# Routed expert rows on one Trainium2 core: fetches that wait for fewer scatters, and padding rows moved from behind each list to ahead of it

## The chip, the cores and the metric

One core of one Trainium2 chip runs the kernel. The metric is the device time of one execution in microseconds (us). A core has five engines that matter here: TensorE (PE, matmuls; its weight loads are listed as PEld), VectorE (DVE), ScalarE (ACT), GpSimd (POOL) and SyncE (SP). Each engine runs its own instructions strictly in the order in which the program holds them, and waits for others at semaphores. SP computes nothing here: it issues most of the DMA transfers. POOL issues the DMAs whose row addresses are computed on the chip.

## The reference

```
# x: 8 x 3584 tokens of 192;  weight_gen: 8 heads x 7 taps for each token
w = softmax(weight_gen, axis=-1)
x = einsum('bshk,bskhg->bshg', w, windows(x_pad, 7))   # causal mix of 7 tokens
x = x.reshape(N, D)                                     # N = 28672, D = 192

xn = x / (norm(x) + 1e-6);  en = expert_emb / (norm(expert_emb) + 1e-6)
logits = xn @ en.T / tau                                # 8 experts
expert_idx = argmax(logits);  gate_w = softmax(logits)[expert_idx]
for e in range(8):
    mask = expert_idx == e
    h = maximum(x[mask] @ w1[e], 0)                     # 192 -> 1024
    out[mask] = gate_w[mask] * (h @ w2[e])              # 1024 -> 192
```

Each token goes through one expert alone, so the kernel sorts the tokens by expert before the two large matmuls.

## The kernel before

**Chunks.** The 28672 tokens are worked in 16 chunks of 1792 (14 groups of 128). For each chunk SP loads the tokens (`x_t`, two loads of 1248 KB) and the tap weights (`w_t`, 392 KB); DVE and ACT mix the seven taps; the chunk's rows (`row`) are turned by a transposing DMA (`xT<-row`), TensorE forms the logits (`g_ps`), and DVE finds each token's expert and its place (`pos`) in that expert's list. Then POOL writes the chunk's rows into the lists with 14 indirect DMAs, the scatters (`lst<-row,pos`, 128 rows of 776 bytes each, L590). `lst` lies in DRAM: a region of REG = N + 256 rows for each of the 8 experts, and a few rows of zeros behind them all (row DUMMY and on), which a tile reads that has nothing to do. `run` holds for each expert where the next row goes, `used` where the next row to be read lies.

**Tiles.** With each of the chunks 0 to 14 go eight tiles, one for each expert, of 128 or 256 rows (`sizes`, L25): 120 tiles, numbered here from 0, so that chunk c has tiles 8c to 8c+7. `schedule` (L612) decides on DVE whether the expert's list has enough rows by then. Behind them come 45 "last" tiles of 128 rows, whose experts and rows a plan on the chip picks (class `Plan`, around L836) from what the lists still hold. A tile's fetch (`load_rows` and `fetch`, L643 to L661) is three steps on SP: read the first row's number from `sched` into a register (TENSOR_LOAD), a transposing DMA `xt<-lst`, and a small DMA `meta<-lst` with the gates and token numbers. There are three `xt` buffers (`XBUFS`), so a fetch waits at least until TensorE has done the first matmuls of the tile three before it. TensorE then does `first` (`h_ps<-xt,wall`), ACT and DVE the two halves of the ReLU (`hi`, `lo`), TensorE `second` (`acc<-wall,hi` and `lo`), ACT scales, and POOL stores the tokens' results (`out_dram<-o,meta`).

**Order.** The program is emitted by a planner (`run_steps`, L942) that holds costs and priorities for steps; a framework adds the semaphores from the tiles and the DRAM tensors that instructions touch. It sees `lst` as one tensor. So the kernel takes dependences away by groups: scatters are in the group "rows", fetches in the group "loads", and an instruction can be declared free of a whole group. In the kernel before, scatters are declared free of both groups, while a fetch keeps its dependence on every scatter that the program emitted ahead of it, of its own chunk or of a later one.

**Padding.** A last tile always reads 128 rows, so it can reach beyond its list's end. `pads` (L1346) writes 256 rows of zeros behind each list's last row when the last chunk has been placed: eight times a register load and a DMA of 194 KB on SP, ahead of the last tiles' fetches. At the very start `pad_rows` (L1055) writes the rows at DUMMY. A fallback behind the program (from L1480) takes what 45 last tiles did not; it is not run with these inputs.

Of the kernel before, what the change touches and what calls it, by code (L numbers as in the profile page):

```python
# [11 lines left out]
I32 = mybir.dt.int32  # L12
AF = mybir.ActivationFunctionType
ALU = mybir.AluOpType
# [78 lines left out]
def tile_dynconv_moe(  # L93
# [535 lines left out]
    class Tile:  # L629
# [13 lines left out]
        def load_rows(self, row0, deps):  # L643
            def fetch():
                return self.fetch(nc.sync.value_load(row0, min_val=0, max_val=DUMMY))

            for i in SP.behind(fetch):
                i = raw_ins(i)
                tc.add_to_no_dep_group("loads", i)
                for d in deps:  # L650
                    tc.add_manual_dep(i, d.name, sync_dep, reason="rows of the lists")

# [129 lines left out]
    class Plan:  # L782
# [27 lines left out]
        def make(self):  # L810
            E1 = E + 1
            jt, ji = self.take(M), self.take(M, dt=I32)
            G_.iota(ji, pattern=[[1, M]], base=0, channel_multiplier=0)
            G_.tensor_copy(out=jt, in_=ji)
            left, lefti = self.take(E), self.take(E, dt=I32)
            V.tensor_tensor(out=left, in0=run[0:1, :], in1=used, op=ALU.subtract)
            yield
            V.tensor_scalar(out=lefti, in0=left, scalar1=float(P - 1), scalar2=None, op0=ALU.add)
            yield
            V.tensor_scalar(  # L820
                out=lefti, in0=lefti, scalar1=P.bit_length() - 1, scalar2=None, op0=ALU.logical_shift_right
            )
            yield
            V.tensor_copy(out=left, in_=lefti)
            ends = self.take(E1)
            V.memset(ends[:, 0:1], 0.0)
            yield
            V.tensor_tensor_scan(
                out=ends[:, 1:], data0=left, data1=zero_t[0:1, 0:E], initial=0.0, op0=ALU.add, op1=ALU.add
            )  # L830
            yield
            past = self.take(M, E1)
            V.tensor_tensor(
                out=past, in0=jt.unsqueeze(2).broadcast_to([1, M, E1]), in1=ends.unsqueeze(1).broadcast_to([1, M, E1]),
                op=ALU.is_ge,
            )  # L836
            first = self.take(E)
            yield
            V.scalar_tensor_tensor(out=first, in0=ends[:, 0:E], scalar=-float(P), in1=used, op0=ALU.mult, op1=ALU.add)
            mine = self.take(M, E)  # L840
            yield
            V.tensor_tensor(out=mine, in0=past[:, :, 0:E], in1=past[:, :, 1:], op=ALU.subtract)
            ex = self.take(M)
            yield
            V.tensor_reduce(out=ex, in_=past[:, :, 1:], axis=AX.X, op=ALU.add)
            self.experts = self.take(M, dt=I32)
            yield
            V.tensor_scalar(out=self.experts, in0=ex, scalar1=float(E - 1), scalar2=None, op0=ALU.min)
            num = self.take(E)
            yield  # L850
            V.tensor_reduce(out=num, in_=mine.rearrange("p m e -> p e m"), axis=AX.X, op=ALU.add)
            yield
            V.scalar_tensor_tensor(out=used, in0=num, scalar=float(P), in1=used, op0=ALU.mult, op1=ALU.add)
            yield
            V.tensor_tensor(out=mine, in0=mine, in1=first.unsqueeze(1).broadcast_to([1, M, E]), op=ALU.mult)
            rows = self.take(M)
            yield
            V.tensor_reduce(out=rows, in_=mine, axis=AX.X, op=ALU.add)

            yield  # L860
            V.tensor_scalar(
                out=jt, in0=jt, scalar1=float(P), scalar2=-float(DUMMY), op0=ALU.mult, op1=ALU.add
            )
            yield
            V.scalar_tensor_tensor(out=jt, in0=past[:, :, E], scalar=-1.0, in1=jt, op0=ALU.add, op1=ALU.mult)
            self.rows = self.take(M, dt=I32)
            yield
            V.scalar_tensor_tensor(
                out=self.rows, in0=rows, scalar=float(DUMMY), in1=jt, op0=ALU.add, op1=ALU.subtract
            )  # L870
# [16 lines left out]
    e_i = prep.tile([P, E], I32, name="e_i")  # L887
    G_.iota(e_i, pattern=[[1, E]], base=0, channel_multiplier=0)
    V.tensor_copy(out=rev[:, 0, :], in_=e_i)
    V.tensor_scalar(out=run, in0=rev[:, 0, :], scalar1=float(REG), scalar2=None, op0=ALU.mult)  # L890
    V.tensor_scalar(out=rev, in0=rev, scalar1=-1.0, scalar2=float(E), op0=ALU.mult, op1=ALU.add)
    V.tensor_copy(out=used, in_=run[0:1, :])
    wlast = prep.tile([P, WC], F16, name="wlast")
# [23 lines left out]
    def add(eng, cost, fn, deps=(), key=(), dma=0.0, lat=1.0):  # L917
        s = Step(eng, cost, fn, [d for d in deps if d is not None], key, dma, lat)
        steps.append(s)
        return s  # L920
# [134 lines left out]
    def pad_rows():  # L1055
        for r in range(DUMMY, DUMMY + TAIL, P):
            SP.dma_start(out=lst[r : r + P, :], in_=pad)

    L["pads"] = add("SP", 1.0, pad_rows, (), (0, 5), 0.6)

    def taus():
# [281 lines left out]
            t.needs = ([L["parts", e, 0], L["parts", e, 1]], [L["low", e]])  # L1343
            tile_graph(t, (lambda t=t: t.load(scheds[c], routes[c].rows), L["scatter"  , c] + [L["sched", c][-1], L["pads"]]), c)

    def pads(deps):  # L1346

        ends = sm.tile([1, E], I32, name="ends")
        V.tensor_copy(out=ends, in_=run[0:1, :])
        yield  # L1350
        for e in range(E):

            def put():
                r = nc.sync.value_load(ends[0:1, e : e + 1], min_val=e * REG, max_val=e * REG + N)
                return SP.dma_start(
                    out=lst[bass.ds(r, TAIL), :].rearrange("(s p) c -> p s c", p=P),
                    in_=pad.unsqueeze(1).broadcast_to([P, TAIL // P, ROW // 2]),
                )

            i = raw_ins(SP.behind(put))  # L1360
            tc.declare_no_dep(i, group="rows", reason="behind the last token's row")
            tc.declare_no_dep(i, group="loads", reason="behind the rows that are read")
            tc.add_to_no_dep_group("rows", i)
            deps.append(i)

    def last_batch():
        c = NCH - 1
        deps = []
        box = []

        def start():
            box.append(Plan())
            deps.extend(routes[c].rows)
            return box[0].make()

        free_ = [L["taps", (c, u)][-1] for u in range(2)]
        free_ += L["split", (c, 1)] + L["scatter", c] + [L["logits", 2 * c + 1]]
        rows_at = chain(
            lazy(lambda: pads(deps)), [("V", 0.08), ("SP", 8.0)], [last_places(c)[2], L["pads"]], (0, -1, c)
        )  # L1380
        rows_at[1].dma = 0.6
        mk = chain(
            lazy(start), [("V", x) for x in (0.1, 0.08, 0.08, 0.12, 0.08, 0.36, 0.08, 0.33, 0.33, 0.1, 0.33, 0.08, 0.33, 0.33, 0.1, 0.1, 0.1)], [last_places(c)[-1], L["sched", c - 1][-1]] + free_, (1, c, 5)
        )
        nb = 3
        cps = []
        for j in range(M):
            lasts.append(LastBox())
            t = lasts[j]
            t.j = j  # L1390
            k0 = [mk[9], mk[16]]
            prev = cps[-1:]
            old1 = [tile_steps[TB + j - nb]["first"][-1]] if j >= nb else free_
            old2 = [tile_steps[TB + j - nb]["second"][-1]] if j >= nb else free_
            c1 = add("V", 1.12, lambda t=t: t.copy(0), k0 + prev + old1, (1, c, 6, j))
            c2 = add("V", 0.85, lambda t=t: t.copy(1), k0 + [c1] + old2, (1, c, 6, j))
            cps += [c1, c2]
            t.needs = ([c1], [c2])
            t.start(box)
            tile_graph(t, (lambda t=t: t.load(box[0], deps), L["scatter", c] + [mk[16], rows_at[1]]), c)  # L1400

    class LastBox:

# [48 lines left out]
    def fetch_first():  # L1452
# [17 lines left out]
    total = sm.tile([1, 1], F32, name="total")  # L1470
    V.tensor_reduce(out=total, in_=left, axis=AX.X, op=ALU.add)
    lefti = sm.tile([1, E + 1], I32, name="lefti")
    V.tensor_scalar(out=lefti[:, 0:E], in0=left, scalar1=float(TAIL - 1), scalar2=None, op0=ALU.add)
    V.tensor_copy(out=lefti[:, E:], in_=total)
    V.tensor_scalar(
        out=lefti[:, 0:E], in0=lefti[:, 0:E], scalar1=TAIL.bit_length() - 1, scalar2=None, op0=ALU.logical_shift_right
    )
    nexti = sm.tile([1, E], I32, name="nexti")
    V.tensor_copy(out=nexti, in_=used)
    some = nc.values_load(lefti[0:1, E : E + 1], min_val=0, max_val=N)  # L1480
    with tc.If(some > 0):
        for e in range(E):
            n = nc.values_load(lefti[0:1, e : e + 1], min_val=0, max_val=N // TAIL)
            r0 = nc.sync.value_load(nexti[0:1, e : e + 1], min_val=e * REG, max_val=e * REG + N)
            with tc.For_i(0, n, 1) as i:
                t = Tile(e, TAIL)
                t.fetch(nc.s_assert_within(r0 + i * TAIL, e * REG, e * REG + N))
                for g in range(t.ng):
                    t.first(g)
                    t.relu(g)  # L1490
# [58 lines left out]
```

## Time and profile before

| | |
|---|---|
| median of 3 runs | 1243.48 us (1241.87 to 1247.8) |
| profiled execution, its own time | 1246.79 us |
| its span in the trace | 1245.0 us |
| mean granted clock of TensorE | 0.987 |
| PE busy | 1177.2 us (95%) |
| DVE busy | 1066.5 us (86%) |
| ACT busy | 776.1 us (62%) |
| POOL busy | 624.3 us (50%) |

The span is the time from the first to the last instruction of the profiled execution, and the execution's own time is 1.8 us more. Busy time is counted for each engine by itself; issuing DMAs does not count as busy, so SP has no row. A granted clock below 1 means that the hardware let TensorE run at less than its full speed for a part of the time.

### The profile page before, as it was taken

Reading aid. Unit: us, or ns where it says so; the run is one execution under the profiler, and the core shown is the slowest. Engines: PE = TensorE matmul, PEld = TensorE weight load, DVE = VectorE, ACT = ScalarE, POOL = GpSimd, SP = SyncE. Lnnn points to the kernel's source line nnn. Section 1 sums busy time; section 2 is a strip of 40 time slices with the busy share of each in tenths; the row PEclk is TensorE's granted clock in tenths of the full one; section 3 lists DMA queues with packets and bytes.
Section 4 is the critical chain, followed back from the end, with each engine's and each line's share of the span. In section 5 each row is a group of like instructions: output and inputs, shape, how many; then the busy total and the mean of one; then the engine's idle time right before and its main releaser. Section 6 shows DMA issues by size and latency. Waiting matters only on the chain.

```text
span 1245.0 us, 34972 instructions
## 1 busy us (share of the span) xinstructions
PE 1177.2 (95%) x13600; PEld 1050.8 (84%) x13600; DVE 1066.5 (86%) x1505; ACT 776.1 (62%) x1938; POOL 624.3 (50%) x498
## 2 busy tenths in 40 slices
PE   2999979899999999999999899989999999999997
PEld 1554459799988989999898899989999999999997
DVE  5998899799989998999899899988899447778784
ACT  1398867668787877788677678655455533333332
POOL 1006334547555674848284746584848463333332
PEclk9999999999999999999999999999999999999999
DMA  9644554758386747655656657365554541222221
GB/s 368 261 105 119 154 134 113 157 121 181 114 173 160 176 120 162 165 123 152 129 141 139 163 129 176 107 164 128 124 106 98 110 136 46 48 48 50 45 45 32
DMA packets 273487, 162.56 MB, mean 131 GB/s; under 512 B 249493, under 2 KB 258957, under 8 KB 268192
## 3 DMA queue, kind: packets, MB, share of 16 engines
q1 hardware_dynamic: 250416, 101.26, 36.7%
q0 software_dynamic: 21744, 44.30, 11.9%
q10 hardware_dynamic: 1152, 14.68, 2.8%
q8 instruction: 108, 1.77, 0.6%
q14 instruction: 67, 0.55, 0.2%
HBM read 62.24 MB, written 46.55 MB: 87 GB/s over the span
## 4 chain that ended last, share of the span: by engine, by line
PE 57%; DMA 13%; issue 12%; DVE 10%; POOL 6%; ACT 1%; POOLq 0%; SPq 0%; ACTq 0%; DVEq 0%
PE h_ps L78 28%; PE acc L78 22%; DMA lst<-row,pos 5%; PE sums L78 5%; POOL out_dram L78 4%; DMA xT<-row 3%; DVE acc L78 3%; DVE prod L78 3%; POOL lst L78 2%; DMA xt<-lst 2%; DMA out_dram<-o,meta 1%; PE less L78 1%; DMA w_t<-in_weight_gen_dram 1%; PE g_ps L78 1%; DVE lo L78 1%
## 5 line engine op out<-in xcount | busy, mean ns | idle before, releaser
L78 POOL DMA_INDIRECT out_dram<-o,meta x229 | 302.3, 1320 | 407.5 <-ACT o L78 363.6
L78 PE MATMUL h_ps<-xt,wall 128*128 128x256 f16 (+1 forms) x4800 | 458.5, 250 | 26.3 <-DMA xt<-lst 26.3
L78 PEld LDWEIGHTS <-wall 128*128 128x128 f16 (+1 forms) x4996 | 397.3, 99 | 70.8 <-DMA xt<-lst 23.1
L78 ACT ACTIVATE hi<-h_ps 128x512 f16<-128x512 f32 x458 | 272.6, 596 | 266.3 <-PE h_ps L78 190.1
L78 POOL DMA_INDIRECT lst<-row,pos x224 | 313.0, 1397 | 190.1 <-ACT sq L78 95.9
L78 PE MATMUL acc<-wall,hi 128*128 128x192 f16 x2944 | 390.7, 247 | 0.0
L78 PE MATMUL acc<-wall,lo 128*128 128x192 f16 x1472 | 363.4, 247 | 0.0
L78 PEld LDWEIGHTS <-hi 128*128 128x128 f16 x3664 | 330.8, 98 | 17.9 <-issue 0.8
L78 DVE TENSOR_TENSOR prod<-x_t,w_t 128x1344 f32<-128x1344 f32 x178 | 276.1, 1551 | 5.5 <-PE sums L78 3.3
L78 DVE TENSOR_TENSOR acc<-acc,prod 128x1344 f32<-128x1344 f32 x162 | 251.6, 1553 | 2.4
L78 DVE SCALAR_TENSOR_TENSOR lo<-h_ps,hi 128x512 f16<-128x512 f32 x230 | 153.5, 683 | 41.6 <-ACT hi L78 41.6
L78 PEld LDWEIGHTS <-lo 128*128 128x128 f16 x1832 | 179.8, 98 | 0.1
L78 ACT ACTIVATE lo<-h_ps 128x512 f16<-128x512 f32 x228 | 133.7, 594 | 52.3 <-PE h_ps L78 51.5
L78 ACT ACTIVATE o<-acc,meta 128x192 f32<-128x192 f32 x229 | 89.5, 420 | 64.6 <-PE acc L78 54.3
L78 ACT ACTIVATE acc<-acc,sc 128x192 f32<-128x192 f32 x224 | 90.8, 450 | 0.5
L78 ACT ACTIVATE sq<-acc 128x192 f16<-128x192 f32 x224 | 80.9, 361 | 7.0 <-DVE acc L78 4.3
L78 PE MATMUL h_ps<-hi,minus 128*128 128x512 f16 x228 | 84.6, 383 | 0.0
L78 PE MATMUL h_ps<-xt,x_t 128*128 128x128 f16 x1200 | 76.8, 219 | 0.0
L78 PE MATMUL sums<-acc,io_i 128*128 128x448 f32 x114 | 50.7, 584 | 23.1 <-DVE enorm L78 21.1
L78 DVE TENSOR_TENSOR acc<-x_t,w_t 128x1344 f32<-128x1344 f32 x46 | 71.1, 1548 | 1.2 <-PE sums L78 1.1
L78 PEld LDWEIGHTS <-x_t 128*128 128x128 f16 x1200 | 71.1, 98 | 0.0
L78 DVE TENSOR_TENSOR row<-acc,row 128x896 f16<-128x896 f32 x64 | 52.7, 852 | 13.0 <-ACT row L78 12.5
(147 smaller groups left out, 1052.1 us busy)
## 6 DMA issues: line engine op xcount, KB each, us to landing
x_t<-in_x_dram SPq DMA_DIRECT2D x32, 1248.0 KB
wall<-in_moe_w_dram ACTq DMA_DIRECT2D x7, 1792.0 KB
w_t<-in_weight_gen_dram SPq DMA_DIRECT2D x16, 392.0 KB
out_dram<-o,meta POOLq DMA_INDIRECT x229
lst<-row,pos POOLq DMA_INDIRECT x224
xt<-lst SPq DMA_TRANSPOSE x165
wlast<-in_moe_w_dram ACTq DMA_DIRECT2D x1, 1792.0 KB
meta<-lst SPq DMA_DIRECT2D x101, 1.0 KB
```

What stands on the lines that cost most here:

```text
L78: self.last = self.tc.keep_in_program_order(op(*args, **kwargs))
```

## The change

A fetch is declared free of the group "rows", except for the scatters that it names itself, those of its own chunk. Each list now begins 128 rows into its region (`run` starts at e*REG + 128). The last tiles are counted from a list's end: tile j of an expert reads the 128 rows that end 128*j rows ahead of the list's last row, so that the one that doesn't fill up reaches back into rows that were already worked (and writes their results again) or into the 128 rows ahead of the list. Those are filled with zeros by one DMA, `front_rows` (128 x 8 x 194 words, 794 KB), which keeps a dependence on the last scatter of chunk 8; `pads` and its eight DMAs are gone. The planner gives `front_rows` out behind the fetch of tile 76 and the scatters of chunk 8. The fallback goes in tiles of 128 instead of 256.

```
@@ load_rows
             for i in SP.behind(fetch):
                 i = raw_ins(i)
                 tc.add_to_no_dep_group("loads", i)
+                tc.declare_no_dep(
+                    i, group="rows", keep=list(deps), reason="later rows lie behind those that are read"
+                )
                 for d in deps:
                     tc.add_manual_dep(i, d.name, sync_dep, reason="rows of the lists")
@@ Plan
-            V.scalar_tensor_tensor(out=first, in0=ends[:, 0:E], scalar=-float(P), in1=used, op0=ALU.mult, op1=ALU.add)
+            V.scalar_tensor_tensor(
+                out=first, in0=ends[:, 0:E], scalar=float(P), in1=run[0:1, :], op0=ALU.mult, op1=ALU.add
+            )
...
-    V.tensor_scalar(out=run, in0=rev[:, 0, :], scalar1=float(REG), scalar2=None, op0=ALU.mult)
+    V.tensor_scalar(out=run, in0=rev[:, 0, :], scalar1=float(REG), scalar2=float(P), op0=ALU.mult, op1=ALU.add)
@@ behind pad_rows
+    def front_rows():
+        i = raw_ins(
+            SP.behind(
+                SP.dma_start,
+                out=lst[0:DUMMY, :].rearrange("(e r) c -> r e c", e=E)[0:P],
+                in_=pad.unsqueeze(1).broadcast_to([P, E, ROW // 2]),
+            )
+        )
+        r = routes[8].rows[-1]
+        tc.declare_no_dep(i, group="rows", keep=[r], reason="ahead of the first token's row")
+        tc.declare_no_dep(i, group="loads", reason="ahead of the rows that are read")
+        tc.add_manual_dep(i, r.name, sync_dep, reason="in the middle of the run")
+        tc.add_to_no_dep_group("rows", i)
+        front.append(i)
@@ last_batch (def pads is removed)
-            deps.extend(routes[c].rows)
+            deps.extend(routes[c].rows + front)
...
-        rows_at = chain(
-            lazy(lambda: pads(deps)), [("V", 0.08), ("SP", 8.0)], [last_places(c)[2], L["pads"]], (0, -1, c)
-        )
-        rows_at[1].dma = 0.6
+        fronts = add("SP", 1.0, front_rows, [L["pads"], tile_steps[76]["fetch"]] + L["scatter", 8], (1, 76, 1), 0.6)
...
-            tile_graph(t, (lambda t=t: t.load(box[0], deps), L["scatter", c] + [mk[16], rows_at[1]]), c)
+            tile_graph(t, (lambda t=t: t.load(box[0], deps), L["scatter", c] + [mk[16], fronts]), c)
```

The programs' own order shows two places on SP. A wait on DMASW with a number is one for a DMA that POOL issued (a scatter or a store), on DMAHW for one that SP issued, on PE, DVE or Activation for that engine. The first place is tiles 75 to 77 of chunk 9, before: the end of tile 75's fetch, the next chunk's two loads, and the fetches of tiles 76 and 77.

```order
L78 DMA meta<-lst 128x2 [waits DMAHW7_49]
L78 DMA x_t<-in_x_dram 128x2496 [waits DVE_49]
L78 DMA w_t<-in_weight_gen_dram 128x784 [waits DMAHW1_49]
L645 TENSOR_LOAD sched
L645 ISA x2
L78 ISA
L78 DMA_TRANSPOSE xt<-lst 128x3x128 [waits DMAHW2_49,DMASW6_49,PE_49]
L78 ISA
L78 DMA meta<-lst 128x2 [waits DMAHW3_49,DMASW5_49,DMASW4_49]
```

The same place of the changed kernel:

```order
L78 DMA meta<-lst 128x2 [waits DMAHW0_49]
L78 DMA x_t<-in_x_dram 128x2496 [waits DVE_49]
L78 DMA w_t<-in_weight_gen_dram 128x784 [waits DMAHW2_49]
L645 TENSOR_LOAD sched
L645 ISA x2
L78 ISA
L78 DMA_TRANSPOSE xt<-lst 128x3x128 [waits DMAHW3_49,PE_49]
L78 ISA
L78 DMA meta<-lst 128x2 [waits DMAHW4_49,DMASW5_49,DMASW4_49]
```

The order is the same, and the transposing fetch has lost its wait on DMASW6, a scatter of chunk 10. The second place is tiles 58 to 60 of chunk 7, before: the end of tile 58's fetch, a load of tokens, tile 59's fetch, the tap weights of the chunk after next, tile 60's fetch.

```order
L78 DMA meta<-lst 128x2 [waits DMAHW3_49]
L78 DMA x_t<-in_x_dram 128x2496 [waits DMAHW4_49,DVE_49]
L645 TENSOR_LOAD sched
L645 ISA x2
L78 ISA
L78 DMA_TRANSPOSE xt<-lst 128x3x128 [waits DMAHW5_49,DMAHW6_49,DMASW2_49,PE_49]
L78 ISA
L78 DMA meta<-lst 128x2
L78 DMA w_t<-in_weight_gen_dram 128x784 [waits DMAHW7_49]
L645 TENSOR_LOAD sched
L645 ISA x2
```

The same place of the changed kernel, where the DMASW1 of the padding write is chunk 8's last scatter:

```order
L78 DMA meta<-lst 128x2 [waits DMAHW3_49]
L78 DMA x_t<-in_x_dram 128x2496 [waits DMAHW4_49,DVE_49]
L645 TENSOR_LOAD sched
L645 ISA x2
L78 DMA lst<-pad 128x8x194 [waits DMAHW5_49,DMASW1_49]
L78 ISA
L78 DMA_TRANSPOSE xt<-lst 128x3x128 [waits DMAHW6_49,PE_49]
L78 ISA
L78 DMA meta<-lst 128x2 [waits DMAHW7_49]
L78 DMA w_t<-in_weight_gen_dram 128x784 [waits DMAHW0_49]
L645 TENSOR_LOAD sched
```

Tile 59's fetch has lost its wait on DMASW2, an earlier scatter of chunk 8, and the padding write stands ahead of it: the framework has placed that DMA 18 fetches ahead of where the planner emitted it.

## Rows read from the trace of the kernel before

**Rows 1.** The page: span, and busy time of the engines.
```profile
span 1245.0 us, 34972 instructions
PE 1177.2 (95%) x13600; PEld 1050.8 (84%) x13600; DVE 1066.5 (86%) x1505; ACT 776.1 (62%) x1938; POOL 624.3 (50%) x498
```

**Rows 2.** Windows: stretch and length, busy time by engine, granted clock, DMA share, GB/s.
```profile
core 0: us, PE busy (x) PEld busy (x) DVE busy (x) ACT busy (x) POOL busy (x), PEclk, DMA share, GB/s
250.00:1050.00 800.00, 781.23 (x9165) 724.70 (x9164) 712.62 (x943) 544.75 (x1409) 480.88 (x378) 0.99 0.58 137
700.00:710.00 10.00, 8.55 (x95) 8.12 (x96) 5.85 (x10) 3.85 (x8) 8.30 (x8) 0.83 0.62 119
1000.00:1050.00 50.00, 50.00 (x567) 47.70 (x565) 29.20 (x51) 18.67 (x37) 25.67 (x28) 1.00 0.39 105
```

**Rows 3.** Waits of PE and of SP: total us, times, longest.
```profile
PE h_ps L78 <- DMA xt<-lst: 26.3, 10, 5.7
SPq L78 <- DMA lst<-row,pos: 230.4, 38, 11.7
```

**Rows 4.** Timeline of PE: start, us, instruction, [idle before <- what ended it].
```profile
357.14 1.07 PE L78 MATMUL h_ps<-xt,wall 128*128 128x128 f16 x16 [2.30 <-DMA xt<-lst]
...
464.07 1.12 PE L78 MATMUL h_ps<-xt,wall 128*128 128x128 f16 x17 [1.39 <-DMA xt<-lst]
...
576.64 1.07 PE L78 MATMUL h_ps<-xt,wall 128*128 128x128 f16 x16 [0.88 <-DMA xt<-lst]
...
701.45 1.21 PE L78 MATMUL h_ps<-xt,wall 128*128 128x128 f16 x10 [4.03 <-DMA xt<-lst]
...
826.66 1.01 PE L78 MATMUL h_ps<-xt,wall 128*128 128x128 f16 x15 [3.11 <-DMA xt<-lst]
...
838.34 0.83 PE L78 MATMUL h_ps<-xt,wall 128*128 128x256 f16 x6 [0.92 <-DMA xt<-lst]
...
851.17 0.69 PE L78 MATMUL g_ps<-enT,xT 128*128 128x16 f16 x21 [1.16 <-DMA xT<-row]
```

**Rows 5.** Timeline of SP around tile 29's fetch.
```profile
346.34 0.43 SPq L78 DMA_DIRECT2D x_t<-in_x_dram  x1
346.81 0.43 SPq L78 DMA_DIRECT2D w_t<-in_weight_gen_dram  x1
348.06 1.80 SPq L78 DMA_TRANSPOSE xt<-lst  x1
```

**Rows 6.** The chain that ended last: start, us, what.
```profile
281.25 4.48 DMA lst<-row,pos
...
348.06 9.03 DMA xt<-lst
...
448.84 2.88 DMA lst<-row,pos
...
567.13 6.87 DMA lst<-row,pos
```

**Rows 7.** Timeline of SP: loads ahead of tiles 43, 76 and 94, and tile 76's fetch.
```profile
454.00 0.39 SPq L78 DMA_DIRECT2D x_t<-in_x_dram  x1
...
689.17 0.44 SPq L78 DMA_DIRECT2D x_t<-in_x_dram  x1
...
698.27 1.21 SPq L78 DMA_TRANSPOSE xt<-lst  x1
...
814.78 0.45 SPq L78 DMA_DIRECT2D x_t<-in_x_dram  x1
```

**Rows 8.** Timeline of SP around tile 59's fetch.
```profile
565.45 0.37 SPq L78 DMA_DIRECT2D x_t<-in_x_dram  x1
574.05 1.21 SPq L78 DMA_TRANSPOSE xt<-lst  x1
...
575.92 0.44 SPq L78 DMA_DIRECT2D w_t<-in_weight_gen_dram  x1
```

**Rows 9.** Timeline of POOL: the issue of chunk 8's last scatter.
```profile
578.03 0.97 POOL L78 DMA_INDIRECT lst<-row,pos  x1 [0.30 <-issue]
```

**Rows 10.** The tile `pad`: issues, ns min/median/max, first and last start.
```profile
L78 SPq DMA_DIRECT2D lst<-pad x10: 372/380/427, 3.1 to 1012.2; - x10
L78 SPq MOVE lst<-pad x8: 29/29/29, 1003.1 to 1012.2; - x8
```

More of the change, by code (lines that the diff above doesn't have):

```diff
@@ L852, in make @@
             yield
-            V.scalar_tensor_tensor(out=used, in0=num, scalar=float(P), in1=used, op0=ALU.mult, op1=ALU.add)
+            V.scalar_tensor_tensor(
+                out=run[0:1, :], in0=num, scalar=-float(P), in1=run[0:1, :], op0=ALU.mult, op1=ALU.add
+            )
             yield
@@ L861, in make @@
             V.tensor_scalar(
-                out=jt, in0=jt, scalar1=float(P), scalar2=-float(DUMMY), op0=ALU.mult, op1=ALU.add
+                out=jt, in0=jt, scalar1=-float(P), scalar2=-float(DUMMY + P), op0=ALU.mult, op1=ALU.add
             )
@@ L1057, in pad_rows @@
             SP.dma_start(out=lst[r : r + P, :], in_=pad)
+    def front_rows():
[5 more added lines that the diff above has]
+            )
+        )
+        r = routes[8].rows[-1]
[4 more added lines that the diff above has]
+        front.append(i)
+    front = []
     L["pads"] = add("SP", 1.0, pad_rows, (), (0, 5), 0.6)
@@ L1344, in batch @@
             tile_graph(t, (lambda t=t: t.load(scheds[c], routes[c].rows), L["scatter"  , c] + [L["sched", c][-1], L["pads"]]), c)
[L1346 to L1357, printed above, removed]
-                )
[L1360 to L1364, printed above, removed]
     def last_batch():
@@ L1377, in last_batch @@
         free_ += L["split", (c, 1)] + L["scatter", c] + [L["logits", 2 * c + 1]]
-        rows_at = chain(
-            lazy(lambda: pads(deps)), [("V", 0.08), ("SP", 8.0)], [last_places(c)[2], L["pads"]], (0, -1, c)
-        )
-        rows_at[1].dma = 0.6
+        fronts = add("SP", 1.0, front_rows, [L["pads"], tile_steps[76]["fetch"]] + L["scatter", 8], (1, 76, 1), 0.6)
         mk = chain(
@@ L1472, in tile_dynconv_moe @@
     lefti = sm.tile([1, E + 1], I32, name="lefti")
-    V.tensor_scalar(out=lefti[:, 0:E], in0=left, scalar1=float(TAIL - 1), scalar2=None, op0=ALU.add)
+    V.tensor_scalar(out=lefti[:, 0:E], in0=left, scalar1=float(P - 1), scalar2=None, op0=ALU.add)
     V.tensor_copy(out=lefti[:, E:], in_=total)
     V.tensor_scalar(
-        out=lefti[:, 0:E], in0=lefti[:, 0:E], scalar1=TAIL.bit_length() - 1, scalar2=None, op0=ALU.logical_shift_right
+        out=lefti[:, 0:E], in0=lefti[:, 0:E], scalar1=P.bit_length() - 1, scalar2=None, op0=ALU.logical_shift_right
     )
     nexti = sm.tile([1, E], I32, name="nexti")
-    V.tensor_copy(out=nexti, in_=used)
+    V.tensor_copy(out=nexti, in_=run[0:1, :])
     some = nc.values_load(lefti[0:1, E : E + 1], min_val=0, max_val=N)
@@ L1482, in tile_dynconv_moe @@
         for e in range(E):
-            n = nc.values_load(lefti[0:1, e : e + 1], min_val=0, max_val=N // TAIL)
-            r0 = nc.sync.value_load(nexti[0:1, e : e + 1], min_val=e * REG, max_val=e * REG + N)
+            n = nc.values_load(lefti[0:1, e : e + 1], min_val=0, max_val=N // P)
+            r0 = nc.sync.value_load(nexti[0:1, e : e + 1], min_val=e * REG, max_val=e * REG + P + N)
             with tc.For_i(0, n, 1) as i:
-                t = Tile(e, TAIL)
-                t.fetch(nc.s_assert_within(r0 + i * TAIL, e * REG, e * REG + N))
+                t = Tile(e, P)
+                t.fetch(nc.s_assert_within(r0 - (i + 1) * P, e * REG, e * REG + N))
                 for g in range(t.ng):
```

## The prediction, on record before the changed kernel ran

> **What bounds the kernel now.** I read the page first. TensorE is busy for 1177.2 of 1245.0 us, DVE for 1066.5 [rows 1]: TensorE bounds, and what a change of waits can win is TensorE's idle time. The windows say where that lies. From 250 to 1050 us TensorE is busy for 781.23 of 800 us, 18.8 idle, and DVE for 712.62, so DVE has 87 us of slack there. From 1000 to 1050 TensorE is busy for 50.00 of 50 [rows 2]: nothing is to be won at the end, where the old padding writes stand. Then the waits of TensorE: 26.3 us for fetches, ten times, the longest 5.7 [rows 3]. SP waited for scatters for 230.4 us, 38 times [rows 3]; nearly all of it is hidden behind three buffers, since TensorE's whole wait for fetches is a ninth of it. So I went through TensorE's timeline and kept the gaps that begin on SP with a wait for a scatter, or behind one: 2.30 us ahead of tile 29, 1.39 ahead of 43, 0.88 ahead of 59, 4.03 ahead of 76, 3.11 ahead of 94, 0.92 ahead of 96, and 1.16 ahead of logits whose turn stood behind those last fetches [rows 4]. The first fetches of the run (5.7 us the longest) wait for their own chunk's rows and stay.
>
> A long gap costs more than itself: in 700 to 710 us, behind the 4.03 us, the granted clock is 0.83 against 0.99 over the long stretch [rows 2, 4], so about 1.7 us of work were lost to a lower clock.
>
> **The waits that go.** At tile 76 the loads of the next chunk went out at 689.17 and the fetch only at 698.27 [rows 7]; its buffer was not what it waited for, and in the new order its wait on a scatter is gone. But the gain isn't the whole wait, because the fetch now falls right behind the two loads in SP's own queue. Tile 29 shows what that costs: x_t out at 346.34, w_t at 346.81, the fetch at 348.06 [rows 5], and it took 9.03 us to land [rows 6], so 10.75 us from x_t's issue. A fetch that waits for the scatters took 2.59 us (574.05 to TensorE's start at 576.64) [rows 4, 8].
>
> The low bound leaves x_t where it is. Then tile 43 lands at 454.00 + 10.75 = 464.75 and wins nothing against 464.07; tile 76 lands at 699.9 and wins 1.5 of its 4.03; tile 94 at 825.5 and wins 1.1 of 3.11 [rows 4, 7]; tiles 29, 96 and the turn win nothing. Sum 2.6 us. The high bound is all gaps but tile 59's, 2.30 + 1.39 + 4.03 + 3.11 + 0.92 + 1.16 = 12.9 us, and the clock behind the two long ones, 2 x 1.7: 16.3 us. I take 15, near the upper: the fetches ahead of x_t lose their waits on scatters too (SP's 38 waits lie in front of all of them), so x_t and w_t go out earlier by what their buffers allow, and two or three us earlier are enough for 29, 43 and 94. DVE's 87 us of slack are more than the 15.
>
> **The padding write.** It is one DMA of 794 KB, but it doesn't stand where the planner put it. In the new order it stands on SP ahead of tile 59's fetch, and it waits for chunk 8's last scatter. POOL issued that one at 578.03 [rows 9]; SP's fetch 59 went out at 574.05 [rows 8], after a wait for an earlier scatter of the same chunk (issued 567.13, 6.87 us to land, behind the x_t load of 565.45) [rows 6, 8]. SP is in order. So this fetch, which TensorE already waited for, loses one wait and gets a later one. Behind it are queued the w_t load (575.92 before) [rows 8], which DVE's next softmax needs, and the fetches 60 to 62.
>
> The cost by steps. Landing of the scatter: nothing large is ahead of it, 2.88 to 4.48 us as two others in the chain [rows 6], so 580.9 to 582.5; I take 581.6. The issue of a padding write takes 0.38 us [rows 10], so the fetch goes at 582.1 (581.4 to 583.0). Landing: 2.59 us if the padding doesn't hold it up. From above: at tile 29 1640 KB held a fetch, issued 1.72 us behind, for 9.03 - 2.59 = 6.44 us, so they held the queue for 8.2 us [rows 5, 6]; 794 KB by proportion for 4.0, less 0.5 that the fetch comes later, 3.45. I take 3.0, near the upper end, for it is the same queue. TensorE's start of tile 59 is then 587.7 (584.0 to 589.0) against 576.64: 11.1 us later (7.4 to 12.4). Behind a gap of 12 us the clock falls as behind 4.03: 1.7 us, and at most I take double; 2.5 in the sum. Together 13.6 us (9.1 to 15.8). DVE can't make up for it by going ahead, as its own load comes as late.
>
> The Trainium skill (DMA: Bandwidth & Descriptors, section on the anatomy of one DMA, SWDGE path) fits a DMA's time as about 2.0 us plus its bytes at 436 GB/s. An estimate by that fit for 794 KB is 1.9 us of moving; the sum would be 1.1 us better. By the same fit tile 29's 1640 KB hold the queue for 3.9 us, where the rows give 8.2, so I go by the rows; the fit was made for another path than SP's.
>
> **What costs nothing.** The eight old padding writes stand on SP from 1003.1 to 1012.2, 9.1 us [rows 10], in a stretch in which TensorE is never idle [rows 2]; taking them away wins nothing. Should the fetches behind them be the ones that TensorE waits for, it would be at most those 9.1 us. The changed sums in the plan are as many DVE instructions as before. The last tiles are as many and as large. The new fetches read rows that need no further wait, since the padding has landed hundreds of us before.
>
> **Sum.** On the profiled execution: -15 + 13.6 = -1.4, from 1246.79 to 1245.4 us. That execution is 3.3 us above the median of 1243.48, so I forecast **1242 us**. With the ends of both terms against each other this case reaches from -7 (16.3 won, 9.1 lost) to +6 (10 won, 15.8 lost). What a measurement here can tell from no change is 0.5%, 6.2 us: the bounds are 1237.3 and 1249.7. The forecast is no change that can be told, out of two terms that are each larger than that.
>
> **Rivals.**
> The padding write holds up nothing that counts (0.18). This would be so if it were issued without a long wait, with chunk 8's scatters landed by the time SP comes to it, or if TensorE had other work there. Against it: the gap of 0.88 at 576.64 says that TensorE had used up its work [rows 4], and the scatter's issue at 578.03 is later than that [rows 9]. For it: POOL and DVE get ahead if SP's loads and turns do. The gain is then left alone: 1243.5 - 15 = 1228.5 us.
> Slower: the waits for scatters are only exchanged for waits behind x_t and w_t (0.26). The place is the fetch right behind the two loads, once in each chunk; the price is the 10.75 us from x_t's issue. It decides if the loads don't go out earlier, because the fetch ahead of them still waits for its buffer until then. Then the gain is 2.6 and the loss stays: +11, 1254.5 us. For it: a scatter that took 6.87 us was itself late behind x_t [rows 6, 8], so the same transfer delays both, and a fetch in the same queue no less. Against it: tile 76's fetch had nine us between its loads and itself [rows 7], and SP waits 38 times, not once in a chunk [rows 3].
> The forecast's own case has 0.56; of that 0.10 lies under 1237.3 and 0.02 over 1249.7.
>
> **Range and chances.** Faster by over 0.5%: 0.18 + 0.10 = 0.28. Slower: 0.22 of the second rival and the 0.02 = 0.24. Within: 0.48. The forecast's own range is 1236 to 1249; to leave no more than 2 in 10 out it reaches to the middle of each rival, 1228 to 1255.
>
> **What the profile would show.** SP's timeline: a long stretch without an issue ahead of lst<-pad near 581, then fetch 59 within one us; TensorE idle for about 12 us ahead of tile 59, and a granted clock clearly under 1 in the ten us behind. If that gap is under 3 us, the first rival is right. SP's wait for scatters well under 230 us. Gaps ahead of the tiles 29, 43, 76, 94 under 1 us; if tiles 76 and 94 still show 2 us and more, and their fetches take 8 us and more to land, the second. At 1003 no padding and TensorE without a gap, as before. What would make me wrong beyond this: a gap at a new place, where SP comes to a turn or a chunk's first fetch earlier than DVE or the own scatters are ready, and TensorE, now further ahead, has less work in store.

## The result, and the profile after

| | before | after |
|---|---|---|
| median | 1242.67 us (4 runs) | 1224.93 us (4 runs, 1224.13 to 1228.26) |
| ratio after/before | | 0.9858 (95%: 0.982 to 0.9896) |
| span of the profiled execution | 1245.0 us | 1226.5 us |

The change made the kernel 1.4% faster, 17.7 us, where no change that can be told was forecast; the time lies under the forecast range of 1228 to 1255 us. The page of the changed kernel, span and busy times, and then its waits of PE: total us, times, longest.

```profile
span 1226.5 us, 34932 instructions
PE 1171.9 (96%) x13600; PEld 1046.2 (85%) x13600; DVE 1063.8 (87%) x1504; ACT 774.1 (63%) x1938; POOL 632.0 (52%) x498
```

```profile
PE h_ps L78 <- DMA xt<-lst: 16.4, 6, 10.6
PE g_ps L78 <- DMA xT<-row: 0.3, 1, 0.3
```

TensorE's waits for fetches fell from 26.3 us [rows 3] to 16.4, and one wait alone makes 10.6 of these. Here it is, in the timeline of PE (start, us, instruction, [idle before <- what ended it]), with the two gaps near tiles 14 and 65 that are left:

```profile
238.34 1.29 PE L78 MATMUL h_ps<-xt,wall 128*128 128x128 f16 x20 [0.25 <-DMA xt<-lst]
...
572.20 2.31 PE L78 MATMUL h_ps<-xt,wall 128*128 128x128 f16 x20 [10.63 <-DMA xt<-lst]
606.37 0.69 PE L78 MATMUL g_ps<-enT,xT 128*128 128x16 f16 x21 [0.29 <-DMA xT<-row]
```

The gaps of [rows 4] at tiles 29, 43, 76 and 94 are gone. The one at tile 59, 0.88 us before, is 10.63 us. POOL and SP show why, as their timelines answer to [rows 8] and [rows 9]:

```profile
563.84 0.97 POOL L78 DMA_INDIRECT lst<-row,pos  x1 [0.30 <-issue]
```

```profile
550.60 0.37 SPq L78 DMA_DIRECT2D x_t<-in_x_dram  x1
566.25 0.40 SPq L78 DMA_DIRECT2D lst<-pad  x1
566.83 2.04 SPq L78 DMA_TRANSPOSE xt<-lst  x1
```

Chunk 8's last scatter was issued at 563.84, the padding write went out 2.4 us later, SP had issued nothing for 15 us, and tile 59's fetch followed right behind. SP's only wait from 550 to 567 is the one for that scatter:

```profile
SPq L78 <- DMA lst<-row,pos: 14.6, 1, 14.6
```

TensorE got to tile 59 at 572.20, 5.4 us behind that fetch, where it took 2.59 before [rows 4, 8]; the padding held the fetch for 2.8 us. The window of the ten us behind the gap (length, busy time of PE, PEld, DVE, ACT, POOL, granted clock, DMA share, GB/s) shows the lower clock:

```profile
571.70:581.70 10.00, 9.50 (x108) 9.01 (x109) 5.12 (x6) 5.94 (x16) 2.01 (x2) 0.75 0.27 76
```

So the loss was there as forecast. What was not forecast is that the kernel was already far ahead when it came to this place. Where TensorE gained is read by taking the time of each tile's first matmul in both traces, and the difference of the differences from tile to tile. At tile 58 TensorE was 14.2 us earlier than before (572.16 against 557.96), while the forecast knew up to there of the gaps at tiles 29 and 43 alone, 3.7 us. Most of the difference is in the first 20% of the run: from tile 12 to tile 15 TensorE gained 8.6 us (253.61 against 244.51 at tile 15, 230.54 against 230.06 at tile 12). There the kernel before had the gap that I had left out, as the timeline of PE shows it, and a low clock behind, as the window shows:

```profile
244.65 1.57 PE L78 MATMUL h_ps<-xt,wall 128*128 128x128 f16 x13 [5.68 <-DMA xt<-lst]
```

```profile
244.60:252.00 7.40, 7.35 (x80) 6.70 (x81) 3.63 (x7) 2.18 (x5) 0.99 (x1) 0.57 0.69 116
```

The reader is to see in this that 5.68 us of idle time are followed by 7.4 us at a clock of 0.57, which loses another 3.2 us, so this one gap is worth about 9 us.

### The profile page after: what moved, and what is told of

Same layout as the page of the kernel before. It is cut to its first block, busy times and chain, and to the rows that moved or that the text cites. A ratio compares the mean times of both kernels' runs of the same rounds, so it can differ in the third digit from the quotient of the medians.

```text
span 1226.5 us, 34932 instructions
## 1 busy us (share of the span) xinstructions
PE 1171.9 (96%) x13600; PEld 1046.2 (85%) x13600; DVE 1063.8 (87%) x1504; ACT 774.1 (63%) x1938; POOL 632.0 (52%) x498
## 4 chain that ended last, share of the span: by engine, by line
PE 73%; DVE 9%; issue 7%; DMA 6%; POOL 4%; ACT 1%; POOLq 0%; SPq 0%; ACTq 0%; DVEq 0%
PE h_ps L78 35%; PE acc L78 29%; PE sums L78 6%; POOL out_dram L78 3%; DVE acc L78 3%; DVE prod L78 2%; DMA lst<-row,pos 2%; PE less L78 2%; PE g_ps L78 1%; DMA w_t<-in_weight_gen_dram 1%; POOL lst L78 1%; DMA xT<-row 1%; DMA xt<-lst 1%; DMA out_dram<-o,meta 1%; DVE w_t L78 1%
## 5 line engine op out<-in xcount | busy, mean ns | idle before, releaser
L78 POOL DMA_INDIRECT out_dram<-o,meta x229 | 308.2, 1346 | 379.7 <-ACT o L78 306.6
L78 PE MATMUL h_ps<-xt,wall 128*128 128x256 f16 (+1 forms) x4800 | 453.5, 248 | 16.4 <-DMA xt<-lst 16.4
L78 PEld LDWEIGHTS <-wall 128*128 128x128 f16 (+1 forms) x4996 | 393.2, 98 | 60.0 <-DMA xt<-lst 13.9
L78 PE MATMUL sums<-acc,io_i 128*128 128x448 f32 x114 | 52.5, 601 | 22.5 <-DVE enorm L78 20.6
L78 DVE TENSOR_TENSOR row<-acc,row 128x896 f16<-128x896 f32 x64 | 52.5, 851 | 10.4 <-ACT row L78 10.2
```

The source lines that it names most:

```text
L78: self.last = self.tc.keep_in_program_order(op(*args, **kwargs))
```

## The experiments

Each was timed against the kernel before on the same chip; the ratio is that of the times.

**The fetches' waits alone.** The kernel before with one piece of the change:

```
             for i in SP.behind(fetch):
                 i = raw_ins(i)
                 tc.add_to_no_dep_group("loads", i)
+                tc.declare_no_dep(
+                    i, group="rows", keep=list(deps), reason="later rows lie behind those that are read"
+                )
```

> The kernel before with the first part of the change alone: a fetch waits for its own chunk's scatters only; the eight old padding writes and the plan stay. Theory A (the removed waits win about 31 us, 9 of them already ahead of tile 16, and the padding write gave 12 back at tile 59, of which some 5 were recovered at the next turn): 1243 - 31 + 5 = about 1216, no gap above 1 us ahead of tile 59, and a gap of about 3 us for the turn's logits near tile 65 again. Theory B (a good part of the gain is from the new plan and the dropped padding writes): above 1228. Theory C (the stall at tile 59 cost nothing net, since it only stands where the next wait on the turn and DVE would stand): about 1225, as the changed kernel.

Measured: 1214.7 us against 1242.21, ratio 0.979 (0.9741 to 0.984). This is theory A's time, 10 us under the whole change. The timeline of PE has no gap at tile 59; near tile 14 and at the turn near tile 65 it shows:

```profile
234.36 0.84 PE L78 MATMUL h_ps<-xt,wall 128*128 128x128 f16 x12 [0.98 <-DMA xt<-lst]
...
590.50 0.69 PE L78 MATMUL g_ps<-enT,xT 128*128 128x16 f16 x21 [1.38 <-DMA xT<-row]
```

The window of the middle of the run, columns as above:

```profile
250.00:1030.00 780.00, 777.23 (x9220) 723.21 (x9218) 708.50 (x946) 542.06 (x1402) 486.28 (x379) 1.00 0.61 140
```

TensorE is busy for 777.23 of 780 us there at a clock of 1.00: the removed waits win all that there was to be won in this stretch. DVE, at 708.50 of 780, did not become the bound. Theory B falls. The expectation erred in one thing: the gap of the turn near tile 65 did not come back at 3 us, it is 1.38. Before, it was

```profile
611.30 0.69 PE L78 MATMUL g_ps<-enT,xT 128*128 128x16 f16 x21 [2.96 <-DMA xT<-row]
```

So that one also came from the scatter waits in part. The traces of the further experiments below that have no stall at tile 59 divide the same way: 2.99 and 2.38 us where those fetches keep their waits, 1.05 to 1.43 where they don't.

**The padding alone.** The changed kernel with that same piece taken out, so that all fetches wait as before.

> The changed kernel with the fetches' old waits put back: only the padding ahead of the lists and the new counting of the last tiles. Theory A: the padding write waits for chunk 8's last scatter ahead of tile 59's fetch, a gap of 10 to 12 us there at the lower clock behind it, and some 5 us recovered at the next turn: 1243 + 7 = about 1250, between 1247 and 1256. Theory B: below 1240. Theory C: 1243, a gap at tile 59 and as much less idle time behind it.

Measured: 1253.68 us against 1242.21, ratio 1.0095 (1.007 to 1.0121), 11.5 us slower and inside theory A's bounds. SP's and PE's timelines have the same picture as the whole change:

```profile
564.98 0.37 SPq L78 DMA_DIRECT2D x_t<-in_x_dram  x1
579.97 0.40 SPq L78 DMA_DIRECT2D lst<-pad  x1
580.57 2.04 SPq L78 DMA_TRANSPOSE xt<-lst  x1
```

```profile
585.94 1.35 PE L78 MATMUL h_ps<-xt,wall 128*128 128x128 f16 x11 [10.66 <-DMA xt<-lst]
```

By the medians almost none of it was recovered behind tile 59, less than the 5 us that theory A had put there. The two traces say otherwise. Counted from tile 58, this kernel is 11.6 us later than the kernel before at tile 60 and 7.1 at tile 119, so 4.5 us came back, 3.0 of them between tiles 64 and 65 (12.01 us against 15.01), where the turn's gap of 2.96 us is 1.34 here. The profiled execution of the kernel before is over 4 us slower than its median, so how much is recovered when the old waits stay is left open. With the two halves apart, -27.5 and +11.5 us add up to -16.0, and the whole change gave -17.7.

**The padding write at its place, without its wait.** In the changed kernel the write waits for tile 58's fetch to land instead of chunk 8's last scatter. The order on SP is the same.

```
-        r = routes[8].rows[-1]
-        tc.declare_no_dep(i, group="rows", keep=[r], reason="ahead of the first token's row")
-        tc.declare_no_dep(i, group="loads", reason="ahead of the rows that are read")
-        tc.add_manual_dep(i, r.name, sync_dep, reason="in the middle of the run")
+        d = fetches[2 * 58]
+        tc.declare_no_dep(i, group="rows", reason="ahead of the first token's row")
+        tc.declare_no_dep(i, group="loads", keep=[d], reason="ahead of the rows that are read")
+        tc.add_manual_dep(i, d.name, sync_dep, reason="behind this fetch")
```

> The changed kernel with the padding write at the same place on SP, but waiting for tile 58's fetch to have landed instead of chunk 8's last scatter. It tells the write's wait from its 794 KB of transfer. Theory A (the wait is the cost): the write goes out near 552, tile 59's fetch at 553 and lands at 559 to 562, the gap ahead of tile 59 is under 1.5 us; 1214 to 1218. If the transfer is the larger cost: a gap of 4 us or more at tile 59 and 1220 or more. Theory C: about 1225 without a gap at tile 59, with new gaps in the 60 us behind it.

Measured: 1215.47 us against 1242.21, ratio 0.979 (0.9745 to 0.9834). SP and PE:

```profile
546.03 0.37 SPq L78 DMA_DIRECT2D x_t<-in_x_dram  x1
547.18 0.40 SPq L78 DMA_DIRECT2D lst<-pad  x1
548.73 2.12 SPq L78 DMA_TRANSPOSE xt<-lst  x1
```

```profile
558.24 0.95 PE L78 MATMUL h_ps<-xt,wall 128*128 128x128 f16 x14 [1.23 <-DMA xt<-lst]
```

The same 794 KB, ahead of the same fetch, cost a gap of 1.23 us. The wait was the main cost, not the transfer: 10.63 us of idle time went to 1.23 when the wait alone was taken away.

**The padding write behind tile 66's fetch.** As the last one, but with both dependences, on the scatter and on tile 66's fetch (`keep=[r]` for the rows, `d = fetches[2 * 66]`).

> The changed kernel with the padding write moved behind tile 66's fetch, where fetches land 12 to 17 us before TensorE needs them. Theory A: no gap at tile 59 and none behind the write; as waits_only, 1213 to 1218, and a gap of about 3 us for the turn near tile 65. Theory C: about 1225.

Measured: 1214.1 us against 1242.21, ratio 0.9771 (0.9723 to 0.9819). The write and tile 67's fetch on SP, and tile 67 on PE, 18.3 us behind its fetch and with no idle time ahead of it:

```profile
594.52 0.39 SPq L78 DMA_DIRECT2D lst<-pad  x1
595.10 2.00 SPq L78 DMA_TRANSPOSE xt<-lst  x1
```

```profile
613.40 0.82 PE L78 MATMUL h_ps<-xt,wall 128*128 128x256 f16 x6
```

Theory C falls with these two: TensorE doesn't meet another wait where the stall was. Against 0.9858 of the whole change, moving or freeing this one DMA is worth 0.7 to 0.9%, 8 to 11 us. This is the version to take: it has the whole change, beats both kernels, and differs from the one before it and from the waits alone by no more than the intervals.

**Where the early gain comes from.** Ahead of tile 14 the trace of before shows no scatter wait at that fetch nor at the one before it. SP's timeline of the kernel before:

```profile
209.46 1.22 SPq L78 DMA_TRANSPOSE xt<-lst  x1
...
215.69 2.17 SPq L78 DMA_TRANSPOSE xt<-lst  x1
...
224.16 1.98 SPq L78 DMA_TRANSPOSE xt<-lst  x1
226.39 0.38 SPq L78 DMA_DIRECT2D meta<-lst  x1
226.81 0.44 SPq L78 DMA_DIRECT2D x_t<-in_x_dram  x1
...
228.53 1.27 SPq L78 DMA_TRANSPOSE xt<-lst  x1
230.06 0.36 SPq L78 DMA_DIRECT2D meta<-lst  x1
230.52 7.63 SPq L78 DMA_TRANSPOSE xT<-row  x1
239.12 1.21 SPq L78 DMA_TRANSPOSE xt<-lst  x1
```

The rows at 209.46, 215.69, 224.16, 228.53 and 239.12 are the fetches of tiles 9, 10, 12, 13 and 14. The first three had waited for chunk 2's scatters, SP's four such waits from 200 to 246 (the fourth, of tile 11, is 0.2 us) being

```profile
SPq L78 <- DMA lst<-row,pos: 11.2, 4, 5.3
```

and all behind them, the loads, the turn and the two fetches, was late. To test this, the waits were taken away (from the kernel before, old padding kept) for some tiles alone: `if self.n < 13:` ahead of the new `declare_no_dep`, and the complement.

> The kernel before, with the scatter waits of later chunks taken from the fetches of tiles 0 to 12 alone (the old padding stays). Theory A (the gaps ahead of tiles 13 and 14, which themselves wait for no scatter, come from the loads x_t and w_t and the turn standing on SP behind the waits of fetches 9, 10 and 12): by tile 16 TensorE is 8 to 9.5 us ahead of the kernel before counted from tile 0's start, nothing behind that; 1232 to 1235. Theory D (those gaps belong to tile 14's own place behind loads and turn, and went for another reason, such as a start that differs from run to run): no change at tile 16, 1240 to 1243.

> The complement: the scatter waits are taken from the fetches of tile 13 and on. Theory A: the gaps of about 5 us ahead of tile 14 stay with the lower clock behind them, all later gains come; 1222 to 1226, and the two halves add up to the gain of taking all waits, 28 us. Theory D: 1213 to 1217, and no gap of 5 us ahead of tile 14.

Measured: for tile 13 and on 1225.22 us against 1243.59, ratio 0.9868 (0.984 to 0.9895), as theory A said, with the gap at tile 14 still there:

```profile
241.06 1.25 PE L78 MATMUL h_ps<-xt,wall 128*128 128x128 f16 x10 [5.28 <-DMA xt<-lst]
```

For tiles 0 to 12 it missed: 1240.89 us, ratio 0.9977 (0.9951 to 1.0003), and a gap at tile 14 that was only less. PE, and SP's wait for scatters from 200 to 246, where four had been:

```profile
239.69 1.57 PE L78 MATMUL h_ps<-xt,wall 128*128 128x128 f16 x13 [3.82 <-DMA xt<-lst]
```

```profile
SPq L78 <- DMA lst<-row,pos: 7.2, 1, 7.2
```

Tile 13's fetch, which had waited for nothing before, now waited 7.2 us. By the semaphores of the trace it waits for a scatter of the same chunk too, the twelfth, a later one than those of tiles 9, 10 and 12. Before, SP came to it 0.9 us after that scatter had landed; now SP came 7 us earlier and met the wait, and the scatter took 6.7 us to land where it had taken 3.1. The turn and tile 14's fetch stood behind that. So the bound was drawn one tile too early, and the next run moved it.

> As the run that took the waits from tiles 0 to 12, but for tiles 0 to 15, so that tile 13's fetch has no scatter wait either. There tile 13's fetch waited 7.2 us for the scatters that 9, 10 and 12 no longer waited for, and the turn and tile 14's fetch stood behind it. Theory A' (of the waits that stand on SP for the same scatters, the first that is left pays, and what is queued behind it is late): tile 13's fetch lands by 230, the gap ahead of tile 14 is under 1 us, by tile 16 TensorE is 8 to 9.5 us ahead, counted from tile 0's start; 1231 to 1235, and with the 18.4 us of the waits from tile 13 on it adds up to the 28 of all. Theory D (tile 14's place behind loads and turn makes its gap, whatever waits): the gap stays over 3 us, 1238 to 1243.

Measured: 1234.55 us against 1241.77, ratio 0.9948 (0.9927 to 0.997). PE at tile 14:

```profile
235.25 1.29 PE L78 MATMUL h_ps<-xt,wall 128*128 128x128 f16 x20 [0.25 <-DMA xt<-lst]
```

The gap went from 5.68 to 0.25 us. Tile 14's fetch on SP:

```profile
231.15 1.20 SPq L78 DMA_TRANSPOSE xt<-lst  x1
```

Counted from tile 8's first matmul (212.39 before, 208.82 here) it goes out at 22.3 us, where it went at 26.7: 4.4 us earlier, less than the 11.2 us of waits, since the freed fetches now wait for their buffers for a part of the time. In the profiled executions tile 16 began 85.5 us behind tile 0 before (172.79 to 258.25) and 76.7 here (169.38 to 246.07), 8.8 us less, as expected. The medians moved by 7.2 us. That and the 18.4 us of tile 13 and on make 25.6, against 27.5 for all waits; both runs free tiles 13 to 15. Theory D falls.

A second early gain lies ahead of tile 0, whose fetch waited for scatters too. SP's wait from 160 to 172 before, then PE at tile 0, before and in the run of the waits alone:

```profile
SPq L78 <- DMA lst<-row,pos: 1.9, 1, 1.9
```

```profile
172.79 1.44 PE L78 MATMUL h_ps<-xt,wall 128*128 128x128 f16 x12 [5.23 <-DMA xt<-lst]
```

```profile
168.95 1.27 PE L78 MATMUL h_ps<-xt,wall 128*128 128x128 f16 x11 [3.57 <-DMA xt<-lst]
```

The three traces in which tile 0's fetch keeps its wait have this wait (1.7 to 1.9 us) and a gap of 5.2 us; the six without it have no such wait and a gap of 3.5 to 3.7.

## Why the prediction was wrong

**The padding write: right.** It stood ahead of tile 59's fetch, it waited for chunk 8's last scatter, its place cost TensorE a gap of 10.63 us where 12 were forecast, the clock behind it 2.5 us where 2.5 were put in (10 us at 0.75), and the kernel without that wait is 8 to 11 us faster, by the traces 12.1 from tile 58 to tile 119 (445.53 us in the run of the waits alone, against 457.62); the sum had 13.6, bounds 9.1 to 15.8. The step on the 794 KB took 3.0 us for the hold of the queue, near the upper end of a proportion from the 1640 KB of tile 29, and measured 2.8. (794 KB counts a KB as 1000 bytes, the 1640 as 1024; in the latter unit the write is 776 KB, which moves the prediction's 4.0 us to 3.9.) The Trainium skill's fit (DMA: Bandwidth & Descriptors, section on the anatomy of one DMA, SWDGE path), by which the prediction estimated 1.9 us, gave too little for SP's queue, as it did for tile 29. In the changed kernel next to nothing made up for it behind, as forecast: from tile 60 to tile 119 it gained 0.9 us on the run of the waits alone (435.56 against 436.45). The first rival, a write that holds up nothing, did not happen, though the time came out under the 1228.5 that it gave.

**The exchange of waits: half right.** Fetches right behind x_t and w_t do land late in the changed kernel (7.3 us at tile 76 and 8.4 at tile 94, by their semaphores, where it was 3.1 and 3.3 before), as the second rival had it, but x_t and w_t went out earlier, and that decided. At tile 76 the loads now stand at 679.67 and the fetch at 682.22, and at tile 94 the fetch goes at 799.97:

```profile
679.67 0.43 SPq L78 DMA_DIRECT2D x_t<-in_x_dram  x1
680.14 0.43 SPq L78 DMA_DIRECT2D w_t<-in_weight_gen_dram  x1
682.22 1.30 SPq L78 DMA_TRANSPOSE xt<-lst  x1
```

TensorE came to tile 76 at 689.90 without a gap that counts. Tiles 29, 43, 76, 94 and 96 and the clock behind them gave about 15 us in the trace of the waits alone, which is what the sum had for them.

**The step that failed** is the sentence "The first fetches of the run (5.7 us the longest) wait for their own chunk's rows and stay." It put these gaps down to the own chunk's scatters, and their gain at nothing. It does not hold even for tile 0: that fetch waited 1.9 us for chunk 1's last scatter, issued at 165.87, while its own chunk's last had been issued at 119.8; in the traces where this fetch is free tile 0's gap is 1.6 us smaller. The longest of these gaps, 5.68 us, is tile 14's. Its fetch waited for no scatter at all, and the prediction did not ask why the loads and the turn ahead of it stood there so late. They stood behind 11.2 us of scatter waits of tiles 9 to 12, all for the next chunk's scatters. Released, tiles 13 to 15 gave 8 to 9 us with the clock, shown by the run to tile 15. In the same way the gap of the turn near tile 65, which the sum left out too, gave about 3 us between tiles 64 and 66 (the shift to before grows from 19.2 to 22.5 us in the trace of the waits alone); that it came from the same waits follows from the traces with and without them, without a run for it by itself. So the gain was 27.5 us where the sum had 15 and its upper bound 16.3. The upper bound was the real mistake: it was built from the gaps that I had traced to a scatter wait, not from all that could be behind one. Idle time and lower clock of the whole stretch would have been the bound: 18.8 us idle from 250 to 1050 [rows 2], the lower clock behind the long gaps there, and before that the gap at tile 14 with its clock, about 9. With the terms as they were measured, 27.5 won and 8 to 11 lost, the sum gives the 17.7 us that were found; the loss was put 3 to 5 us too high, which the forecast's error also holds.

**What costs nothing: right.** With or without the old padding writes, the runs of the waits alone and of the padding behind tile 66 differ by 0.6 us.

**Open.** Tile 0's first matmul begins between 168.9 and 174.8 us in the profiled executions. 1.6 us of that is the wait of its fetch, where it is kept; the rest is there already where the turn ahead of that fetch has been issued, at 164.1 to 168.8 us, and up to there the programs should not differ. Its cause is open. It makes single spans differ by some us, and is one reason why the medians and the traces of an experiment don't agree better. Open, too, is the gap at tile 3, 2.50 us before, which comes and goes in the traces with the waits and without them.

## What to carry to other kernels

On an engine that issues in order, a wait is paid by everything behind it, so a late load or turn with no wait of its own is to be followed back over its queue to the last instruction that did wait. When waits are taken away one by one, the next instruction in the queue that waits for an event of the same kind can meet it, as tile 13's fetch did: take away all of the kind in that stretch, or the gain isn't seen. And a one-off transfer that is freed from its group's dependences should be looked for in the final order, and tied to a place with slack: the same DMA cost 8 to 11 us where it held a late wait ahead of a fetch that TensorE was about to need, and nothing measurable where that wait was over and the next fetch went out 18 us before TensorE needed it.

## What the runs showed of the hardware

The clock's loss did not grow with the gap: 5.68 us of idle time at tile 14 before were followed by 7.4 us at 0.57, 3.2 us lost; 4.03 us at tile 76 by 10 us at 0.83 [rows 2], 1.7 us; 10.63 us at tile 59 after the change by 10 us at 0.75, 2.5 us by that window. Finer windows at tile 59 show why the longest gap did not lose most, columns as above:

```profile
561.60:566.50 4.90, 0.00 (x0) 0.00 (x0) 1.09 (x1) 1.28 (x3) 3.81 (x6) 1.00 0.18 61
566.50:572.20 5.70, 0.00 (x1) 0.01 (x1) 0.00 (x0) 0.00 (x0) 2.87 (x3) 0.50 0.93 251
572.20:576.70 4.50, 4.50 (x34) 4.13 (x35) 2.43 (x2) 1.14 (x4) 0.00 (x0) 0.50 0.39 103
576.70:586.70 10.00, 10.00 (x143) 9.40 (x142) 7.54 (x11) 8.95 (x19) 2.98 (x3) 1.00 0.52 103
```

The clock fell to 0.50, the lower of its two levels (1.2 and 2.4 GHz), while TensorE was still idle. Of the 10.2 us at that level 5.7 lay in the gap, where there was no work to slow down, and only 4.5 behind it, so 2.3 us of work were lost. In the run to tile 15, without the gap at tile 14, the ten us from there on have the full clock:

```profile
235.00:245.00 10.00, 9.75 (x146) 9.28 (x147) 9.86 (x13) 6.47 (x15) 4.58 (x5) 1.00 0.78 142
```

And a DMA that writes 794 KB of padding in rows of 776 bytes on SP's queue held up the next fetch by 2.8 us.
